# A planned instruction order in an SSM-convolution and gMLP kernel: four of six filler groups taken out, and a new order up to the first z tiles

## The chip, the core and the metric

The kernel runs on one core of one Trainium2 chip. The core has a matrix engine (TensorE, PE in the profile), a vector engine (VectorE, DVE), a scalar engine (ScalarE, ACT), a general engine (GpSimd, POOL) and SyncE (SP), which here only issues transfers. Each engine works through its own list of instructions in order; semaphores make one wait for another. Matmuls write to the accumulation memory (PSUM), and the other tiles lie in the on-chip memory (SBUF).

The metric is the device time of one execution, in microseconds. The kernel before takes 311.61 us, the median of three runs (311.52 to 312.55). A profiled execution of it took 311.07 us, and the span from its first to its last instruction is 309.2 us.

## What is computed

One block of a network, on 2048 tokens of width 640 in bf16. Cut to what matters:

```python
mod = (silu(c) @ w_mod).reshape(1, 6, 1, 640)      # sa, ca, ga, sb, cb, gb
h = layernorm(x) * (1 + ca) + sa
kv = shift_conv(k, shift_k) * v                    # 4 taps along the tokens
y = irfft(rfft(pad(kv)) * rfft(pad(ssm_k)))[:2048] + kv * ssm_D
x = x + ga * (h * y)
h = layernorm(x) * (1 + cb) + sb
z = gelu(h @ w_in)                                 # 2 x 864 columns
z1, z2 = z[..., :864], layernorm(z[..., 864:])
g = w_sp @ z2 + b_sp                               # over the 2048 tokens
x = x + gb * ((z1 * g) @ w_out)
```

## The kernel before

The first half (the modulation, the convolution and the first residual) is done in five blocks `u` of 128 columns. The Fourier transforms are matmuls with small tables that the kernel makes itself: M2 for the way forward and G2 for the way back. For each block there are:

- `taps` and `tv`: the four-tap convolution as matmuls with diagonal matrices (16 matmuls for 512 tokens), and DVE's product with v (line 560). K and V of the block are loaded into a `big` tile (`kv0` to `kv4`, two buffers).
- `s1` and `s1c`: the first stage of the transform, and its copies from PSUM. The tiles X1K are those of the filter, X1U those of kv.
- `fwd`: 8 forward stages each for the filter and for kv, of six matmuls. `khc` is ACT's copy of the filter's.
- `prod` (line 463): DVE's products of kv's and the filter's spectra. In half of the stages ("s" in MODE) two operations `csum` (line 477) add them up into W.
- `inv` and `zc`: the inverse stages, and their copies into Z.
- `zt`: a transposing DMA of Z into ZT, issued by SP. Block 4 is turned on PE instead (`zfl`, `zk`).
- `y` and `ym` (line 691), `yl` and `yml` (line 759) in block 4: the last stage, and its product with `gh`. `gh` is the first normalised x (`ln1`, `xn`), multiplied and added by `ghm` (line 674).
- `res` (line 711) adds `gh` to x, and `ln2` (line 717) takes the statistics of the second norm.

The second half works on four groups of 512 tokens. `ag2`, `rstd2`, `nmr2` and `zx` normalise, `hfl` and `hmod` turn and modulate the first group, `turn` and `hmod2` the other three, with a DMA. `zz` are the 64 z products of five matmuls, with `gelu` on ACT, and statistics and a norm of z2 (`stz`, `agz`, `zn`). Then `prodw` multiplies by w_sp, in Strassen's way with sums of halves (`ssum`, `tsum`). The first eighth of that stands in the ordered part; the other seven, with the output projection, follow in plain loops (from line 1160 on).

The ordered part is recorded first. Each step is handed to `op` (line 97), with what it reads and writes. It is one operation or a few, and may be allowed on several engines ("DG" is DVE or GpSimd). `Plan.run` (line 115) then goes through the text ORDER. There each word is an engine's letter (P, A, D, G for GpSimd, S for SP) and a step's number, so ORDER fixes both on which engine a step runs and the order of each engine's list. A step must not stand ahead of what it depends on. No time is in the text.

The modulation's weights `wm0` to `wm5` are loaded by SP into one buffer, one after another. The two halves of w_in (`ldwi`) take over `big` buffers.

The fillers are matmuls whose result is not used:

```python
        for i, k in enumerate(FILLS):
            def fill(e, i=i, k=k):
                p_ = new("fill%d" % i, "s1", [P, S1C, 2 * NJ * 4], F32)
                for j in range(k):
                    mm(p_[:, 0:2], ident[:], ident[:, None, :].to_broadcast([P, S1C, P]), j == 0, j == k - 1)
            op("P", "fill", fill, r=["ident"], w=["fill%d" % i], new=[("fill%d" % i, "s1")], n=k)
```

FILLS has the number of matmuls in each group, of 128 x 512. They are steps 1035 to 1040 before, the last recorded ahead of the final part, so that the steps behind them have numbers lower by four in the kernel after.

Of the kernel before, what the change touches and what calls it, by code (L numbers as in the profile page):

```python
# [30 lines left out]
PE_FLIPS = (4,)  # L31
TB = 4
NQ = DU // 4
FILLS = (4, 6, 2, 2, 4, 3, )
MODE = ('susussus', 'susussus', 'susussus', 'susussus', 'susussus')
SLOTS = dict(Tf=2, W=2, X=4, X1=4, KH=7, T=2, Z=3, ZT=1, wm=1, big=2, dg=2, st1=2, s1=1, sm=2, pu=2, pz=2)
PSUM_TAGS = ("s1", "sm", "pu", "pz")


ORDER = """  # L40
D0 D103 S91 G5 A4 P1035 D13 S2 G104 D105 D118 A1 P7 D119 A120 A10 D6 P8 A121 D106 S92 D14 A16 D107 S23 S25 A11 D94
A108 A109 D15 D17 D93 P1036 P148 A149 D112 D113 A114 G27 A115 D150 P151 G28 A152 P29 D18 D19 P31 P154 A153 A155 D30
D32 D124 G110 D125 A156 P157 A159 A158 D20 S24 P35 S26 D36 P33 D34 A127 A126 D130 G116 G117 G111 P160 A161 S526 G122
P139 D140 S95 D96 P166 A167 A131 P164 A21 D22 A165 G128 G129 P172 A173 G123 P168 A169 G42 P170 A171 D530 D531 S37 S38
P230 P174 A231 P142 P176 D532 P136 S527 A175 A178 A177 D143 G144 D137 P179 A180 P236 A237 S39 G41 S40 P182 G141 D181
A184 D183 P185 D187 A186 D533 P232 A233 P188 D189 P204 P1038 S52 P43 D205 G138 P198 D199 S529 G190 G191 P45 A534 A535
A536 P234 A235 P162 G55 D44 D46 P192 A193 P47 P49 D48 A163 P214 D132 D50 P206 A537 D215 P250 A251 G200 G201 G54 P202
S3 G81 P9 A12 P194 P145 A203 D545 D546 P224 G216 G217 P56 D195 D225 P1040 P1037 S51 P254 P220 A146 P60 A547 A255 D538
A207 P256 G147 A257 P208 P218 D221 G226 G227 S53 D57 A219 S568 P244 D209 G133 G134 A245 A548 P260 A261 D61 P58 D59
G539 D540 D556 D557 P238 P240 A239 P571 A572 S528 D541 D542 D543 S97 D98 G210 G211 P569 A570 P212 A213 P258 P62 P196  # L50
A259 P262 D263 S573 A241 P294 P222 D295 A197 P304 A544 D549 S65 D67 P228 D552 P248 A305 G68 A223 A249 D63 P576 P306
A307 P242 A243 G264 G265 P266 P252 A253 P574 D577 D553 D554 D555 P288 A229 A267 G550 D551 G560 G561 P310 G564 A311
P298 D575 D289 D299 D615 P296 P69 G290 S66 S64 P278 A558 D279 A562 G565 P308 P246 A297 P75 G291 G563 D70 P268 D269
S578 A309 A247 S99 D76 P328 G559 D654 A329 P318 A319 A566 P73 D74 S78 P272 D273 P330 A331 P324 G300 G301 G567 P579
D598 A325 P292 P332 A333 P326 S79 A327 P71 D712 D619 A293 D658 P316 S602 D652 D580 D620 D617 D100 D594 A317 D596 P334
A335 D80 G595 P282 D283 D274 G275 P270 A271 G597 G618 P280 A281 P312 A313 D599 D72 S77 P346 D347 P581 D582 P378 A379
G600 G601 P352 D353 P82 P302 A303 P380 A381 P314 A315 G284 D285 P336 D83 P84 P382 A383 P276 A277 P286 D85 D337 P322
P603 D338 D604 G710 A323 P384 A385 P320 A321 G339 S101 P368 A287 P605 G348 P340 P402 A403 G349 P372 D677 A341 P354
A355 D369 D606 P607 D373 G656 G657 D608 P390 G374 A391 P404 P362 P350 D375 A405 D363 P609 G616 P356 D357 D679 P406
A407 G659 G364 G365 D610 D611 P88 P388 A389 P408 A409 D102 A351 P342 D343 P370 S583 D371 A135 P400 A401 G621 P452 D680  # L60
P376 D89 A453 D622 P386 A387 P392 P86 D87 A377 G675 S623 A393 S90 P410 P456 P366 D411 A457 P398 G358 G359 A367 P624
D625 G612 A399 G412 P360 A361 P416 P454 A455 P420 D417 P626 D627 S759 G413 P414 A415 P394 A395 D421 P458 A459 P628
P344 A345 D629 P442 D443 P630 P476 A477 P430 D431 D432 G655 P418 A419 P396 A397 P482 P466 G613 A467 D631 A483 G422
G423 D642 D644 P446 D447 P424 P426 D427 G433 P434 A425 P478 P436 A479 G637 D641 G632 A435 D676 P444 A445 P460 P480
A481 P428 D437 D448 G449 A461 S660 D634 G653 P661 D662 D635 P474 D633 A429 P584 A475 P663 D664 P468 A585 P484 P450
A469 D485 P665 D666 G438 G439 A451 G673 G674 P440 P464 A441 A465 P500 D501 P667 G486 G487 P520 P488 A489 P504 P502
D521 P462 A463 G714 D505 D640 D668 S586 P587 P470 A471 A503 G522 G506 D507 G523 A588 P490 D491 S681 P510 D511 P508
P524 A509 P494 D495 P492 G711 G678 A525 G512 D513 P472 A493 P682 D683 A473 P516 D517 P514 A515 P684 D685 G496 G497
P498 A499 S760 P518 G669 D636 P686 G713 D638 D687 D639 A519 P722 D645 P688 D689 P718 P724 G670 P720 D719 P726 D721
G690 D691 D692 A723 A725 P728 P729 P727 D730 D731 S589 P592 D732 G695 D761 D733 D762 P1039 P738 D734 D735 P590 D694  # L70
D737 D775 A591 A593 G763 D764 D765 P752 D766 D736 D693 D774 P767 D769 D771 D770 P768 A773 D739 G776 D777 G779 P745
A772 P787 A778 P815 A788 D740 D741 D744 P781 D743 D699 D742 D697 A786 D840 A816 D698 D838 D696 D837 P821 P794 A795
D839 P780 G716 D717 D753 A822 G841 P819 D754 D842 G843 A844 G614 D671 P797 D845 P817 A798 D846 P790 G715 D782 A785
D784 D783 P808 A820 A818 A809 D746 D799 P804 A805 D747 D750 D643 D672 D700 A791 D703 D905 P827 P801 D702 D646 A802
A828 D704 D751 S847 G705 D706 D906 G647 D651 P829 D850 D749 D904 P825 A830 A848 D701 D748 A851 A826 G849 P823 A824
P811 A812 G852 S1042 D903 P881 G907 D908 D909 G910 D757 D813 D806 A882 P853 P856 A857 A854 P889 P883 A890 G912 S1048
D803 A884 P860 P891 A861 A892 P863 A864 P867 A868 D649 P870 D807 S1047 A871 D650 P885 D758 P877 A878 G911 S913 D755
D792 D1052 P895 A886 S1041 D708 D756 A918 A917 P874 A875 P893 P887 D971 A894 D709 D972 A896 D862 D648 D969 D1050 D707
D1053 D970 D789 D793 D865 G973 D974 A975 D976 G914 D915 D916 P933 P919 A934 D796 D800 P936 A888 A920 A937 G978 P943
A944 D1059 P940 P961 D810 D858 A941 P926 A927 A962 D855 D859 G977 S979 A981 P929 P951 D814 G831 D1057 D1058 G982 G984  # L80
D879 D832 D834 A930 A952 D1060 P955 A956 D869 A835 D872 S1045 D938 D935 D866 D939 P922 P949 A950 D980 D942 A923 G983
P1006 P985 A1007 D928 D876 D1049 D873 D921 D931 A986 S1043 P995 A996 D880 G897 P988 A989 D945 D946 D1054 D836 D833
D1065 D924 D898 D932 P1009 P992 D900 A993 D1008 D901 D925 G963 A1010 D987 D990 D1011 D1012 P999 A1000 D1001 D994 S1046
D964 P1002 A1003 D1004 D997 D998 P959 A899 A960 S1044 D991 P1027 D1061 A1028 P1015 A1016 D968 D1005 P947 G1029 A967
D966 A948 P957 A958 D902 P1017 D1066 D1030 D1034 P1023 A1033 A1018 A1024 D965 D1067 D1069 P953 A1031 D1032 D1068 P1073
A954 P1075 P1080 D1070 P1084 D1056 A1074 D1071 D1081 P1077 A1076 P1079 D1072 D1085 P1086 D1078 D1082 D1087 D1055 S1083
P1021 P1013 D1051 A1022 D1063 P1019 A1014 A1020 D1062 D1064 P1025 A1026 S1088
"""


# [39 lines left out]
def kernel(  # L130
# [79 lines left out]
    with ExitStack() as pctx:  # L210
# [748 lines left out]
        for g in range(NT // TB):  # L959
            z_group(g)  # L960
# [5 lines that stand above are left out]
# [258 lines left out]
```

## Time and profile before

| | |
|---|---|
| median of 3 runs | 311.61 us |
| profiled execution | 311.07 us |
| its span | 309.2 us |
| first filler matmul starts | 1.65 us |
| first z product starts | 134.01 us |
| the granted PE clock, mean | 0.999 |
| the w_in halves issued by SP | 94.5 and 117.9 us |

A share of busy time says how long an engine had an instruction running, and a matmul counts as running until its modelled end, which reaches into the next. Start-to-start distances in the timeline are nearer to what an instruction costs. In a line of groups, the first number behind the bar is the busy time and the second the mean duration of one, in ns; behind the second bar stands how long the engine was idle just before them.

### The profile page before, as it was taken

The numbers are of one execution on the slowest core, as the hardware profiler recorded it, in microseconds if no ns is written. First come the engines' busy times: TensorE is split into PE (matmuls) and PEld (weight loads), VectorE is DVE, ScalarE is ACT, GpSimd is POOL, SyncE is SP. The second block draws the span as 40 slices with busy tenths as digits, with TensorE's granted clock in tenths as the row PEclk, the third lists the DMA queues.
The fourth block names the chain that finished last, engine by engine and source line by source line (L and its number), as shares of the span: only waits on it lengthen the run. The fifth ranks groups of instructions, "written<-read, shape, count | busy, mean of one in ns | idle before, by whom it ended". The sixth has DMA issues, their size and how long they took to land.

```text
span 309.2 us, 6893 instructions
## 1 busy us (share of the span) xinstructions
PE 297.1 (96%) x2746; PEld 207.4 (67%) x2746; DVE 260.4 (84%) x531; ACT 156.5 (51%) x278; POOL 120.8 (39%) x152
## 2 busy tenths in 40 slices
PE   6888999999999999999999999999999999999996
PEld 1877888998989898765555555555565656555564
DVE  8999999999998999998799999967675858667473
ACT  4789899986899855466658767040101010010100
POOL 3537565958996698758526411000000000000000
PEclk9999999999999999999999999999999999999999
DMA  8889899998688869105875930093939395640714
GB/s 154 206 189 202 180 273 220 241 179 189 177 136 217 134 151 278 69 2 103 195 115 115 202 81 1 0 139 76 182 92 187 71 168 117 123 102 0 104 30 115
DMA packets 127091, 42.63 MB, mean 138 GB/s; under 512 B 116975, under 2 KB 127060, under 8 KB 127060
## 3 DMA queue, kind: packets, MB, share of 16 engines
q1 hardware_dynamic: 126906, 42.16, 66.3%
q8 instruction: 21, 0.34, 0.5%
q14 instruction: 10, 0.08, 0.1%
q10 hardware_dynamic: 154, 0.05, 0.1%
HBM read 16.11 MB, written 2.62 MB: 61 GB/s over the span
## 4 chain that ended last, share of the span: by engine, by line
PE 69%; DVE 23%; issue 3%; DMA 2%; POOL 2%; ACT 0%; DVEq 0%; POOLq 0%
PE ps L1026 23%; PE pu L244 13%; PE pz L244 11%; PE po L1150 10%; PE sm L244 5%; DVE Tf L463 4%; PE s L244 3%; DVE st L717 3%; PE pz L1026 2%; DMA wm<-in_w_mod_dram 2%; DVE gh L674 2%; PE pu L1026 1%; DVE T L463 1%; DVE xt L711 1%; DVE X L560 1%
## 5 line engine op out<-in xcount | busy, mean ns | idle before, releaser
L244 PEld LDWEIGHTS <-Z 128*128 128x128 bf16 x320 | 31.1, 98 | 27.3 <-DVE Z L910 0.5
L244 PE MATMUL pu<-X,M 128*128 128x128 bf16 (+1 forms) x480 | 46.5, 237 | 2.1 <-ACT KH L247 1.0
L244 PEld LDWEIGHTS <-M 128*128 128x128 bf16 x480 | 37.3, 98 | 6.1 <-issue 2.4
L1032 ACT COPY m<-ps 128x432 f32<-128x432 f32 x7 | 3.6, 518 | 72.7 <-PE ps L1026 72.7
L1026 PEld LDWEIGHTS <-S 128*128 128x128 bf16 x256 | 25.1, 98 | 21.7
L477 POOL TENSOR_TENSOR W<-Tf 128x256 bf16<-128x256 f32 x42 | 31.8, 772 | 13.4 <-DVE Tf L463 9.4
L247 ACT CAST X<-s 128x1024 bf16<-128x1024 f32 x32 | 32.5, 1017 | 6.9 <-PE s L244 6.8
L244 PE MATMUL pu<-big,Z 128*128 128x432 bf16 x160 | 33.3, 346 | 0.2
L1150 PE MATMUL po<-w_o,uT 128*128 128x320 bf16 (+2 forms) x231 | 32.7, 295 | 0.0
L244 PE MATMUL pz<-big,Z 128*128 128x432 bf16 x160 | 32.6, 346 | 0.0
L463 DVE TENSOR_TENSOR Tf<-pu,KH 128x1024 f32<-128x1024 f32 x25 | 30.1, 1213 | 0.6 <-PE pu L244 0.4
L1026 PEld LDWEIGHTS <-wT 128*128 128x128 bf16 x192 | 18.7, 98 | 15.2
L1150 PEld LDWEIGHTS <-uT 128*128 128x128 bf16 (+1 forms) x231 | 22.2, 98 | 9.7
L247 ACT CAST Z<-pz 128x512 bf16<-128x512 f32 x39 | 22.8, 593 | 7.1 <-PE pz L244 6.8
L244 PEld LDWEIGHTS <-G 128*128 128x128 bf16 x330 | 24.8, 98 | 2.1 <-issue 0.6
L247 ACT CAST KH<-pu 128x512 bf16<-128x512 f32 x40 | 23.4, 592 | 4.1 <-PE pu L244 4.1
L1026 PE MATMUL ps<-X,wT 128*128 128x432 bf16 x112 | 22.7, 346 | 0.0
L1026 PE MATMUL ps<-T,S 128*128 128x432 bf16 x112 | 22.7, 346 | 0.0
L244 PEld LDWEIGHTS <-X 128*128 128x128 bf16 x288 | 17.9, 97 | 5.5 <-DVE X L401 2.0
L1026 PE MATMUL ps<-X,S 128*128 128x432 bf16 x112 | 21.6, 346 | 0.0
L244 PE MATMUL sm<-dg,big 128*128 128x128 bf16 x320 | 20.7, 219 | 0.1
L463 DVE TENSOR_TENSOR T<-pu,KH 128x1024 bf16<-128x1024 f32 x15 | 18.2, 1213 | 1.6 <-PE pu L244 1.4
(187 smaller groups left out, 563.2 us busy)
## 6 DMA issues: line engine op xcount, KB each, us to landing
wm<-in_w_mod_dram SPq DMA_DIRECT2D x6, 800.0 KB, 5.4
xt<-in_A_q_dram SPq DMA_DIRECT2D x4, 640.0 KB, 6.0
out_dram<-ot SPq DMA_DIRECT2D x15, 160.0 KB, 2.1
big<-in_B_w_in_dram SPq DMA_DIRECT2D x2, 1080.0 KB, 7.1
X<-in_A_ssm_k_dram SPq DMA_DIRECT2D x4, 512.0 KB, 6.1
big<-in_A_v_dram SPq DMA_DIRECT2D x4, 512.0 KB, 6.3
w_o<-in_B_w_out_dram SPq DMA_DIRECT2D x6, 160.0 KB, 2.7
X<-in_A_ssm_k_dram SPq DMA_DIRECT2D x2, 256.0 KB, 3.4
```

What stands on the lines that cost most here:

```text
L244: nc.tensor.matmul(o, lhsT=w, rhs=x, start=start, stop=stop)
L247: (e.copy if e is nc.scalar else e.tensor_copy)(dst, src)
L463: e.tensor_tensor(T_[:], (tl[pu] if src is None else tl[src])[:, :, :, None, :].to_broadcast(shape), tl[KH][:, :, None, :, :].to_broadcast ...
L477: e.tensor_tensor(tl[W][:, :, o, :], T_[:, :, 0, o, :], T_[:, :, 1, 1 - o, :], op=ALU.add if o else ALU.subtract)
L560: e.tensor_tensor(tl[kv][:].rearrange("p c (n g) -> p n c g", g=8)[:, 4 * i:4 * i + 4], tl[ps][:].rearrange("p a (c g) -> p a c g", g=8), ...
L674: lambda e, vec=vec, o=o: e.tensor_tensor(gvu, gvu, vec[:, None, d0:d0 + du].to_broadcast([P, TB, du]), op=o),
L711: op("GD" if u < NU - 1 else "D", "res", lambda e: e.tensor_tensor(sl, sl, gl, op=ALU.add), r=[("gh", (u, g))], w=[("xt", (u, n)) for n in ...
L717: op("D", "ln2", lambda e, n=n: e.bn_stats(out=st2[:, n, (0, 0, 0, 1, 2)[u], :], in_=xt[:, n, us[0] * DU:(u + 1) * DU]), r=[("xt", (v, n)) ...
L1026: nc.tensor.matmul(ps[:, :FC], lhsT=lhs[:, s_, :], rhs=rhs(s_), start=(s_ == 0 and not more), stop=(s_ == HT - 1), skip_group_check=more)
L1032: nc.scalar.copy(part[p, m][:], part[p, BANK[m]][:, :FC])
L1150: nc.tensor.matmul(ps[:, :hi - lo], lhsT=uTs[t][:fsz[ft], ft, :], rhs=w_o[:fsz[ft], ft, lo:hi], start=(ft == 0), stop=(ft == NFT - 1))
```

## The change

It does two things. FILLS keeps the first two groups alone, so that 2, 2, 4 and 3 matmuls are gone. And ORDER is another one: most steps stand elsewhere, and some on another engine. Its first part, up to the first z tiles, was planned so that DVE's SBUF operations do not begin behind GpSimd's. The rest of the file is the same.

```diff
-FILLS = (4, 6, 2, 2, 4, 3, )
+FILLS = (4, 6)
 ...
-D0 D103 S91 G5 A4 P1035 D13 S2 G104 D105 D118 A1 P7 D119 A120 A10 D6 P8 A121 D106 S92 D14 A16 D107 S23 S25 A11 D94
-A108 A109 D15 D17 D93 P1036 P148 A149 D112 D113 A114 G27 A115 D150 P151 G28 A152 P29 D18 D19 P31 P154 A153 A155 D30
 ...
-D598 A325 P292 P332 A333 P326 S79 A327 P71 D712 D619 A293 D658 P316 S602 D652 D580 D620 D617 D100 D594 A317 D596 P334
 ...
-P498 A499 S760 P518 G669 D636 P686 G713 D638 D687 D639 A519 P722 D645 P688 D689 P718 P724 G670 P720 D719 P726 D721
-G690 D691 D692 A723 A725 P728 P729 P727 D730 D731 S589 P592 D732 G695 D761 D733 D762 P1039 P738 D734 D735 P590 D694
 ...
+A4 A1 D103 S91 S2 D0 S92 S23 G27 S25 G104 P1035 D105 D118 D119 A121 A120 P7 G5 D6 P8 A11 A10 D13 D14 A16 P1036 A28
+D106 D107 A108 D93 D15 D17 P148 A109 A150 A149 P151 D94 A152 A153 D112 D113 A115 A114 P29 P31 P157 D124 A158 D18 D125
 ...
+D580 D595 D597 A562 A563 S602 A333 P312 A313 P324 A131 D132 A325 P334 A335 P581 D100 P326 A327 G567 D621 D622 G284
+D285 P316 A317 D619 P276 A303 D598 D599 P378 A379 P352 P336 P270 D600 G601 G658 D353 S79 A277 D337 P380 A381 P346 D347
 ...
+A591 P592 S760 A593 P767 D769 D770 D771 D740 P768 A772 A773 P745 P797 D741 D743 D777 A778 D696 D699 D744 P794 A779
+P787 A795 A798 D697 D698 G717 D753 P781 A785 A786 D839 G671 P790 G614 D837 D742 D838 D840 P780 A791 D784 D782 D783
```

Steps named in what follows: S602 is the transposed load of ZT0, S79 the load of V for `kv4`, S78 that of its K, S99 a load of the filter's block 3; S760 loads the half of w_in for z1, S589 the last modulation weights; P787 and P797 are z products.

The steps that stand on another engine, in the whole order:

| step | before | after |
|---|---|---|
| `ghm` | 18 on DVE, 22 on GpSimd | 22, 18 |
| `xn` | 6 DVE, 7 GpSimd, 3 ACT | 0, 14, 2 |
| `zx` | 6 DVE, 7 GpSimd, 3 ACT | 6, 4, 6 |
| `zc` | 39 ACT, 1 DVE | 37, 3 |
| `zn` | 11 DVE, 5 ACT | 9, 7 |
| `ln1` | 9 DVE, 7 ACT | 8, 8 |
| `s1c` | 44 ACT, 4 DVE | 43, 5 |
| `gcopy` | 3 DVE, 1 ACT | 4, 0 |
| `diag` | 5 GpSimd | 3 GpSimd, 2 ACT |
| `mneg` | 4 GpSimd | 3 GpSimd, 1 ACT |
| `hmod2` | 4 DVE, 6 GpSimd, 5 ACT | 4, 5, 6 |

`csum` and `res` keep their numbers on each engine, but not the same steps.

## The prediction

> **What bounds the kernel now.** I read the page first, then busy time by stages, then the chain of waits around the seam between the stages, then single instructions.
>
> ```profile
> span 309.2 us, 6893 instructions
> PE 297.1 (96%) x2746; PEld 207.4 (67%) x2746; DVE 260.4 (84%) x531; ACT 156.5 (51%) x278; POOL 120.8 (39%) x152
> PEclk9999999999999999999999999999999999999999
> 0.00:134.00 134.00, 125.08 (x1737) 109.80 (x1738) 127.03 (x244) 104.20 (x183) 92.93 (x120) 1.00 0.85 184
> 134.00:204.00 70.00, 69.82 (x394) 37.31 (x391) 65.01 (x169) 43.77 (x82) 27.92 (x33) 1.00 0.52 95
> 204.00:309.20 105.20, 102.17 (x624) 60.32 (x621) 68.36 (x121) 8.50 (x15) 0.00 (x0) 1.00 0.54 107
> ```
>
> The last three lines are stages; their columns are busy PE, weight load, DVE, ACT, POOL, granted clock, DMA share, GB/s. I cut at 134.0 because the timeline has the first z product of the MLP (five matmuls, `zz`) start at 134.01. From there PE runs without a hole over 0.3 us to 203.9, where the ordered part ends, and the rest of the code is the same in both kernels. So **the change is worth what it does to the start of the first z product**, unless it opens holes after it.
>
> Before 134.0 PE and DVE both look full, which needs a second look.
>
> ```profile
> 130.82 0.29 DVE xt L711
> 131.92 0.71 DVE Z L860 x2
> 133.63 0.72 DVE Z L884 x2
> 142.25 1.12 POOL gh L674
> 147.91 1.45 DVE st L717 x5
> 150.15 1.64 PE pu L244 x8
> ```
>
> This chain of waits (start, length, what) says that what releases PE at the seam is DVE: normalising and modulating the first tokens, then the second group's. For PE I added what matmuls cost by their start-to-start steps: 80 forward stages of 0.44 (35.2), inverse stages 25 x 0.44 + 15 x 0.88 (24.2), 20 taps of 0.89 (17.8), 40 first stages of 0.436 (17.4), 8 modulation rows of 0.68 (5.4), the 21 fillers of 0.2135 (4.5), the rest 12.5: **117.0 us of PE work** before 134.0. It starts at 1.65 and loses 3.9 us before 10 us; 11.4 us more are lost later. DVE, likewise: 40 products of 1.13 (45.2), 20 taps x V of 0.60 (12.0), 16 y products of 0.59 (9.5), nine statistics of 0.99 (8.9), and so on: **117.9 us of DVE work**, from 1.3. DVE's other 14.8 us are two things: 8.6 us by which single operations are longer than the shortest of their kind, and 6.2 us of gaps and short delays.
>
> ```profile
> L674 DVE TENSOR_TENSOR gh<-gh,gca_bf 128x512 bf16<-128x512 bf16 x12 | 4.8, 436 | 0.0
> L674 DVE TENSOR_TENSOR gh<-gh,gsa_bf 128x512 bf16<-128x512 bf16 x5 | 4.0, 795 | 0.0
> 105.80 1.17 DVE L674 TENSOR_TENSOR gh<-gh,gsa_bf 128x512 bf16<-128x512 bf16 x1
> 105.54 1.15 POOL L674 TENSOR_TENSOR gh<-gh,gsa_bf 128x512 bf16<-128x512 bf16 x1
> ```
>
> The first two are groups (count, busy, mean ns): the same shape takes 436 or 795 ns. The last two show why: DVE's began at 105.80, 0.26 us after GpSimd's, and ended 0.28 us after it, in 1.17 us instead of 0.41. That is the loss the new order is about.
>
> **The change part by part.**
> *Fillers.* Eleven of 21 go: 2 at 25.7, 5 at 36.2, 4 at 129.2. By the step, 11 x 0.2135 = 2.35 us of PE work; PE's floor falls to 117.0 - 2.35 = 114.7. They also fill waits: after the five at 36.2 PE still waited 0.4 us, so a part turns into waiting. From nothing to 2.35; I take it together with the order below. The Trainium skill, "TensorE: Matmul & The Clock Gate" (Part 1: The HAM clock gate), speaks against taking them out: an idle window of about 3.4 us halves the clock. Row: the granted clock is 1.00 throughout, the filler's step is 427 ns at 5 us and 216 at 25.7, and the largest hole that the cut can leave is five fillers and their waits, 36.2 to 37.7, 1.5 us. By the row it costs 0; by the rule, if waits merge with it into a cold window, an estimated 1.7 us (3.4 us at half speed) each time. I take 0.
>
> *Operations that change engine before the first z product.* DVE takes 22 modulations of gh instead of 17 (+5 x 0.34 = 1.7), two more Z copies (+1.2), one G copy and one X copy (+1.15), two more residuals (+0.84), one yml (+0.6); it loses six normalisations to GpSimd (-6 x 0.35 = -2.1), one token tile's statistics (-1.0) and three tiny steps (-0.6), two zx (-0.7), two ln2 (-0.65). Sum +0.4: **118.3**. GpSimd's sum goes from 92.6 to 88.5, ACT's from 98.4 to 100.3 (two of its new operations are diagonals of four small copies, with no row on ACT: 0.8 to 2 us each by its steps of 0.21 for the small cosines and 0.48 for half-bank copies, I take 1; it stays 18 us below DVE). Neither sets the end.
>
> *Order.* For each DVE result that a PE stage needs I add DVE's work up to it and PE's work after it. Before, the tightest is the X1U0 copy ahead of the first forward stage of kv: 1.3 + 21.5 + 102.0 = 124.8. After it is 1.3 + 20.3 + 99.6 = 121.2, since the ln1 statistics stand behind the copies and fillers are gone. **Floor -3.6 us**. The actual start lies 9.2 above the floor now (134.0 - 124.8), of which much is the 8.6.
>
> *The stretched operations.* DVE operations with both inputs in SBUF (8 W sums, 17 gh modulations, 4 residuals, 6 additions of D) number 35 before the first z product, with 5.0 of the 8.6 us of stretch, 0.14 each. The new order has 42 of them. The Trainium skill, "SBUF — State Buffer" (Who interferes with whom), says that the pair of ports is an exclusive lock: whichever begins second blocks fully if GpSimd's operation reads SBUF. By that rule, with GpSimd busy 93 of 134 us and half of an operation of about 1.1 us left on average, unplanned would be 42 x 0.69 x 0.55 = 15.9 us (an estimate); by the row 42 x 0.14 = 5.9, and 9.5 with the rest. If the plan holds on the chip, near 0. The listed order doesn't show it: for 26 DVE operations (20 before) it has a GpSimd operation so shortly ahead that by the steps it would still run. Ends: 0 to 15.9; by the nearest row it would be 9.5, and I take half of the 8.6, 4.3, since a plan that separates them can be kept only as far as its starts don't drift.
>
> *SP's queue.* The transposed load of ZT0 moves ahead of the V load of kv4. That load is issued at 64.13 now, ZT0's at 64.75 and holds the queue 7.26 us.
>
> ```profile
> 64.13 0.57 SPq L522 DMA_DIRECT2D big<-in_A_v_dram  x1
> 64.75 7.26 SPq L698 DMA_TRANSPOSE ZT<-Z  x1
> 72.12 1.77 SPq L572 DMA_TRANSPOSE X<-X  x1
> ```
>
> SP now waits until 59.43 to issue X's load ahead of kv4's K; that load is put behind K, so SP can go on from wm0 at 56.7 with K (4.2) and X (0.4) to 61.3, and ZT0 holds it to 68.6, at the latest to 72.0. V lands 4.9 (median) later, 73.5 to 77. Its reader on DVE, at 74.55 now, would come at about 73. Cost 0 to 4 us; behind it on DVE stand all the products. I take 0.5. Of the others, the second w_in load goes behind wm5, needed five z products later (landing 7.1 us; issued about 118, cover 5 us): 0, at most 1. The wm chain (one buffer) is loaded as late as now or later, each about 1 us before its use: 0 to 1.
>
> *After the first z product.* PE has 69.9 us as now. DVE is busy 65 of 70 there, the second group was the late one at 150 (0.28 us). Its DVE work ahead is 131.0 against 130.7, PE's 129.8 against 132.2: it will wait by what DVE still loses, 0 to 2; I take it inside the sum.
>
> **Sum.** DVE: 1.3 + 118.3 + 4.3 + 6.2 = 130.1, against 134.0: -3.9; the V wait +0.5: -3.4, close to the floor's -3.6, got another way (PE's 114.7 and its start of 5.6 leave it 10 us for waits, 11.4 now). Against the profiled execution (311.07 us: span 309.2 and 1.9 around it) that is 307.7; the median of the runs is 0.5 above it, 311.6, so **308.2**.
>
> **Rivals.**
> 1. *The plan holds fully*: stretch 0, -4.3 more; PE's limit, 1.65 + 3.9 + 114.7 = 120.3, is not reached. -7.7: 303.9. For it: the 17 long operations are each over 100 ns, easily avoided. Against it: the list.
> 2. *Only fillers become waits*: stretched operations land elsewhere, DVE's 118.3 is no less than 117.9, so the seam stays at 134 +- 0.7: 311. For it: DVE's work is the same.
> 3. *Slower: the V load of kv4.* SP reaches ZT0 at 64.75 as now, V is issued at 72.0 and takes the 6.5 us of its slowest row: 78.5. DVE, 2 us earlier than now, stands at 72.5 and waits 6.0. Nothing covers it. With the other terms at the row (stretch 9.5, +0.9, and +0.4 of work; the fillers then only fill that wait): +7.3 less the 2 us it had gained and the 2 us of gaps of DVE that the wait swallows: +3.3, 315. It decides from a wait of about 3 us on. Against it: V's median is 4.9 and the new order frees SP earlier.
> That the order does not do what it says is 2 and 3.
>
> **How the numbers follow.** Forecast 0.42 (306 to 310), rival 1 0.18, rival 2 0.12, rival 3 0.28. What can be told from no change is 0.3%, 0.9 us. Faster: 0.42 + 0.18 + 0.01 of rival 2 = 0.61; same 0.09 of it; slower the rest of it and rival 3, 0.30. The range takes rival 1 and reaches to the lower half of rival 3: 302.8 to 314.2.
>
> **What would show it.** The start of the first z product: 130.6 (126.3 with rival 1, 134 with 2, 137 with 3). Of the mean of `gh<-gh,gsa_bf` on DVE: below 500 ns if planned. A DVE wait on the V load at 72 to 79: rival 3. A filler's or matmul's step of twice its length after 10 us: the clock. A hole of over 1 us in PE behind the first z product would make my stage cut wrong.

## The result, and the profile after

The kernel after takes **309.35 us**, the median of ten runs (307.41 to 310.79), where the kernel before took 311.69 in ten runs beside them (311.17 to 312.55). The ratio is 0.9922, with a 95% interval of 0.99 to 0.9944: faster, by about 0.8%. The profiled execution took 309.03 us. Its runs lie further apart than those of the kernel before, 3.4 us against 1.4.

The page of the kernel after (span; busy time; the clock by slices):

```profile
span 306.9 us, 6880 instructions
PE 294.1 (96%) x2735; PEld 206.3 (67%) x2735; DVE 255.9 (83%) x525; ACT 161.9 (53%) x292; POOL 115.3 (38%) x148
PEclk9999999999999999999999999999999999999999
```

PE's share is 96% as before, because the span shrank with the work. In this execution the clock stayed at 1.00. It did not in all of the ten: six have a mean granted clock of 0.999 or 1.000 (median 308.98 us), four have 0.994 (309.95). What lies behind that is told with the fillers below. Where the time went is seen from the stages, in the same columns as above (us from and to; length; busy PE, weight load, DVE, ACT, POOL; granted clock, DMA share, GB/s):

```profile
0.00:131.00 131.00, 121.74 (x1727) 108.52 (x1727) 122.07 (x239) 104.44 (x190) 90.13 (x119) 1.00 0.89 189
131.00:200.00 69.00, 68.12 (x382) 36.36 (x379) 63.53 (x163) 47.87 (x86) 25.15 (x29) 1.00 0.49 93
200.00:307.00 107.00, 104.20 (x635) 61.40 (x633) 70.34 (x125) 9.58 (x17) 0.00 (x0) 1.00 0.52 108
```

The first cut stands at 131.0 because the first z product now starts at 130.99 us, **3.0 us earlier** than at 134.01. DVE was busy 122.1 of the 131.0 us ahead of it, 5 us less than the 127.0 of before. In the second stage PE is busy 68.12 of 69.0 us, where it had been 69.82 of 70.0: holes have appeared there.

The groups that the prediction named, in the stage ahead of the first z product (count | busy us, mean ns of one | idle before):

```profile
L674 DVE TENSOR_TENSOR gh<-gh,gca_bf 128x512 bf16<-128x512 bf16 x12 | 4.8, 415 | 0.0
L674 DVE TENSOR_TENSOR gh<-gh,gsa_bf 128x512 bf16<-128x512 bf16 x10 | 4.4, 444 | 0.1
```

The second group had a mean of 795 ns and is at 444; there are ten of them now instead of five. The plan held on the chip: gate modulations hardly ever begin behind GpSimd's.

What came in its place on DVE is a wait for x (engine, line and tile waited for: us, times, longest), and SP's queue shows why:

```profile
DVE st L593 <- DMA xt<-in_A_q_dram: 1.7, 1, 1.7
```

```profile
23.80 6.96 SPq L525 DMA_TRANSPOSE big<-in_A_k_dram  x1
...
31.86 4.59 SPq L572 DMA_TRANSPOSE X<-X  x1
36.50 0.91 SPq L633 DMA_DIRECT2D wm<-in_w_mod_dram  x1
37.47 0.52 SPq L579 DMA_DIRECT2D xt<-in_A_q_dram  x1
```

Start and length of what SP issues: two transposing loads hold it for 7.0 and 4.6 us, then come the modulation's weights, and only at 37.47 the third quarter of x. That is 1 us earlier than before (38.42), but DVE reached the statistics that read it earlier still. Before, DVE had no wait here.

And ACT's timeline at the seam shows two causes of the holes:

```profile
132.97 1.73 ACT L856 ACTIVATE Z<-xt,nmr,rstd 128x640 bf16<-128x640 bf16 x2 [1.54 <-DVE nmr L846]
134.72 1.28 ACT L933 ACT_TABLE_LOAD   x1
136.02 0.53 ACT L933 ACTIVATE X<-pu 128x432 bf16<-128x432 f32 x1
```

The table for the GELU is loaded at 134.72, between the first z product and the first `gelu`. In the kernel before a step of its own (135, `gelut`) loaded it at 88.03 us, where ACT had time, by a GELU of one column:

```profile
88.03 1.28 ACT L805 ACT_TABLE_LOAD   x1
```

The new order has A135 among the z products, behind the first 18 `gelu` steps, so that the first of these has to load the table itself.

The other cause is the line at 132.97. By the steps of the timeline PE has three holes there, of 0.91, 0.27 and 0.35 us. The first waits for the normalised second pair of token tiles, the other two for the first `gelu` steps (PE's waits, 131 to 140 us):

```profile
PE sm L871 <- ACT Z L856: 0.6, 1, 0.6
PE pu L244 <- ACT X L933: 0.2, 1, 0.2
```

Before, ACT and GpSimd normalised that pair side by side, and it was done 2.1 us behind the start of the first z product. Now ACT does both tiles, one after the other, and it is done 3.7 us behind it.

### The profile page after: what moved, and what is told of

Its sections match the earlier page's. It is cut to its first block, busy times and chain, and to the rows that moved or that the text cites. A ratio compares the mean times of both kernels' runs of the same rounds, so it can differ in the third digit from the quotient of the medians.

```text
span 306.9 us, 6880 instructions
## 1 busy us (share of the span) xinstructions
PE 294.1 (96%) x2735; PEld 206.3 (67%) x2735; DVE 255.9 (83%) x525; ACT 161.9 (53%) x292; POOL 115.3 (38%) x148
## 4 chain that ended last, share of the span: by engine, by line
PE 74%; DVE 14%; DMA 6%; ACT 3%; issue 1%; POOL 1%; DVEq 0%; SPq 0%; POOLq 0%
PE ps L1026 23%; PE pu L244 15%; PE pz L244 14%; PE po L1150 10%; PE sm L244 5%; PE s L244 3%; DVE Tf L463 3%; DMA ZT<-Z 3%; DMA X<-X 2%; PE pz L1026 2%; PE pu L1026 1%; DVE st L717 1%; POOL W L477 1%; DVE st L593 1%; DVE X L560 1%
## 5 line engine op out<-in xcount | busy, mean ns | idle before, releaser
L244 PE MATMUL pu<-X,M 128*128 128x128 bf16 (+1 forms) x480 | 44.9, 237 | 1.4 <-DVE X L247 0.3
L244 PEld LDWEIGHTS <-M 128*128 128x128 bf16 x480 | 36.6, 98 | 5.2 <-issue 1.9
L244 PE MATMUL pu<-big,Z 128*128 128x432 bf16 x160 | 32.6, 346 | 0.3 <-ACT X L933 0.2
L247 ACT CAST Z<-pz 128x512 bf16<-128x512 f32 x37 | 21.9, 596 | 3.3 <-PE pz L244 2.9
L244 PEld LDWEIGHTS <-big 128*128 128x128 bf16 x320 | 18.8, 98 | 0.7 <-issue 0.6
```

The lines of the kernel that those rows point to most:

```text
L244: nc.tensor.matmul(o, lhsT=w, rhs=x, start=start, stop=stop)
L247: (e.copy if e is nc.scalar else e.tensor_copy)(dst, src)
```

## The experiments

**How they are compared.** Two numbers of each profile stand beside the time: the start of the first z product, and the *stretch* of DVE ahead of it, the sum of what its operations took beyond the shortest of their kind (over 0.12 us each; a kind is a line with its tiles and shapes). In this table and in the text that shortest one is taken over all kernels of the table, and so the kernel before has 10.1 us of it. The prediction's 8.6, and the 9.7 of the kernel before without fillers in an expectation, were taken over fewer kernels. The column before the last is the rest of the span behind the first z product; the last one has the number of runs with a mean granted clock of 0.995 or less.

| kernel | median us (runs), ratio to before, 95% | span | first z | stretch | from first z to the end | clock 0.995 or less |
|---|---|---|---|---|---|---|
| before | 311.69 (10) | 309.2 | 134.01 | 10.1 | 175.2 | 0 of 61 |
| after | 309.35 (10), 0.9922, 0.9900 to 0.9944 | 306.9 | 130.99 | 4.5 | 175.9 | 4 of 10 |
| before, no filler groups (e1) | 311.77 (12), 1.0008, 0.9998 to 1.0017 | 310.5 | 135.11 | 11.2 | 175.4 | 4 of 12 |
| after, with filler groups (e2) | 310.01 (6), 0.9950, 0.9933 to 0.9967 | 308.5 | 132.57 | 4.5 | 175.9 | 0 of 6 |
| after, table early (e3) | 308.88 (6), 0.9916, 0.9898 to 0.9933 | 305.7 | 130.16 | 4.6 | 175.6 | 1 of 6 |
| before, three moved (e4) | 310.40 (5), 0.9967, 0.9954 to 0.9980 | 308.8 | 133.42 | 9.5 | 175.4 | 0 of 5 |
| after, table and loads early (e6) | 310.01 (12), 0.9953, 0.9929 to 0.9976 | 309.0 | 133.90 | 4.6 | 175.1 | 8 of 12 |
| after, once more (e7) | 309.09 (6), 0.9927, 0.9908 to 0.9946 | 306.7 | 130.73 | 4.3 | 175.9 | 0 of 6 |
| after, table early, once more (e8) | 308.81 (5), 0.9915, 0.9901 to 0.9929 | 307.2 | 131.82 | 4.1 | 175.4 | 1 of 5 |
| table early, a sum moved (e9) | 309.09 (5), 0.9921, 0.9908 to 0.9935 | 306.9 | 131.54 | 3.7 | 175.4 | 1 of 5 |
| after, three put behind (e10) | 309.77 (12), 0.9937, 0.9914 to 0.9959 | 307.6 | 131.63 | 5.2 | 175.9 | 5 of 12 |
| before's order, after's engines (e11) | 327.95 (6), 1.0532, 1.0506 to 1.0557 | 324.7 | 149.54 | 13.3 | 175.1 | 6 of 6 |
| after's order, before's engines (e12) | 330.05 (5), 1.0608, 1.0584 to 1.0631 | 328.2 | 152.22 | 14.5 | 176.0 | 5 of 5 |

e1 to e4 ran on one chip with the same runs of the kernel before (median 311.58), likewise e7 to e10 (311.47), and e11 and e12 (311.18); e6 ran beside 17 others (311.58). The 61 of the first row are these runs of the kernel before, together.

### The two halves of the change, each alone

e1 takes the four filler groups out of the kernel before and leaves its order. e2 puts them back into the kernel after.

```diff
-FILLS = (4, 6, 2, 2, 4, 3, )
+FILLS = (4, 6)
 ...
-P1037 P1038 P1039 P1040
```

(The words stand at four places of ORDER; e2 is the reverse, and each group stands ahead of or behind the same step as before.)

> The order of before, with the four filler groups taken out and nothing moved. Theory (order): the gain comes from fewer stretched DVE operations, and fillers only stand in time in which PE would wait for DVE anyway, so 311.7 us within 0.6, the first z product at 133.5 to 134.2. Rival (fillers): their 11 x 0.2135 us are work on the path, and the kernel gains 1.5 to 2.4 us, 309.3 to 310.2, which would be all of the change's gain; the first z product then at 131.7 to 132.5.

> The changed kernel with the four filler groups put back, next to the same neighbours where these still follow each other (2 matmuls at about 24 us, 5 ahead of the first stage of block 1's kv, 4 ahead of the second group's last stage at about 125 us). Theory (order): no more than 0.7 us slower than the changed kernel, 309.3 to 310.0. Rival (fillers): 1.5 to 2.4 us slower, 310.9 to 311.7, as slow as before.

**The fillers alone are worth nothing in the median**: 311.77 against 311.58 us, ratio 1.0008. PE lost 18.8 us in waits ahead of the first z product instead of 15.4: more than the 2.35 us of matmuls came back as waits. DVE had nothing less to do, and lost 1.1 us more by stretches, since everything that shifted a little met GpSimd elsewhere. Two of DVE's modulations, which had taken 0.41 and 0.55 us before, in the timeline of this kernel (start, length):

```profile
57.66 0.94 DVE L674 TENSOR_TENSOR gh<-gh,gca_bf 128x512 bf16<-128x512 bf16 x1
...
62.37 1.04 DVE L674 TENSOR_TENSOR gh<-gh,gca_bf 128x512 bf16<-128x512 bf16 x1
```

The first z product came 1.1 us later, as much as the stretch had grown. In the new order the fillers do cost something: with them the first z product is 1.6 us later and the median 310.01 against 309.09 to 309.35 (the second pair in other batches, with intervals that overlap). So **the order carries the gain**, and the cut is worth at most some 0.9 us on top of it.

The fillers did one thing that the medians hide: **they kept the clock up**. In all 72 runs with the six groups (the kernel before, e2 and e4) the mean granted clock is 0.998 or more. Of the 68 runs of after, e1, e3 and e6 to e10, which lack four groups, 24 have 0.989 to 0.995. e1 differs from the kernel before in the fillers alone, and has four of 12 against none of 61. What such a number is, the trace of e6 shows, whose profiled run has 0.989 (stages, the same columns):

```profile
36.61:40.02 3.41, 1.08 (x18) 0.94 (x16) 1.24 (x2) 1.32 (x4) 1.40 (x3) 1.00 1.22 133
40.02:43.43 3.41, 3.41 (x27) 2.92 (x25) 3.31 (x10) 1.50 (x2) 2.10 (x3) 0.50 0.97 294
128.77:132.18 3.41, 2.36 (x62) 1.82 (x59) 3.24 (x13) 1.14 (x3) 1.91 (x4) 1.00 0.00 0
132.18:135.59 3.41, 3.41 (x47) 2.43 (x47) 3.34 (x11) 1.61 (x5) 3.24 (x5) 0.50 0.00 0
```

For two stretches of 3.41 us the granted clock is 0.50, behind stretches in which PE was busy for only 1.08 and 2.36 us. One stretch at half the clock in a span of 307 us makes the mean 0.994 (1 - 0.5 x 3.41 / 307), two make it 0.989. The second lies at the seam, where the four fillers at 129.2 used to stand. The kernel before and the kernel after at that time:

```profile
128.76:132.18 3.42, 3.42 (x72) 2.62 (x70) 3.21 (x14) 0.45 (x2) 1.40 (x3) 1.00 0.02 5
128.76:132.18 3.42, 2.63 (x48) 2.01 (x49) 3.32 (x12) 2.40 (x5) 3.25 (x5) 1.00 0.00 0
```

Laid anywhere at the seam, 3.41 us hold at least 3.12 us of busy PE in the kernel before, 2.57 in e1 and 2.36 in the kernel after. Where the clock fell in the four runs of the kernel after is still not shown, as the trace that was kept is of a run at 0.999, and what exactly the clock goes by is open. By the medians a run with such a stretch is 1.0 us longer in the kernel after (309.95 against 308.98) and 0.5 us in e1 (311.91 against 311.38).

### The table load

e3, and e8 beside a second batch of the kernel after (e7), have one word moved:

```diff
-P400 A401 D677
+P400 A135 A401 D677
 ...
-P883 A884 A135 S1043
+P883 A884 S1043
```

> The changed kernel with one ACT step moved: the one that brings in the Gelu table stands where it stood before (about 88 us, between copies) and not behind the first two gelus. Theory (table): the 1.28 us load at 134.7 us is what holes PE between 134 and 138.8 us (1.5 us lost there against 0.5 before); gone, the kernel gains 0.7 to 1.3 us, 308.0 to 308.7, and the load on ACT at about 86 us is covered. Rival (first tokens late): PE waits there for the normalised second pair of token tiles, which DVE hands to ACT at 132.97, and the load only lies in that wait: no change within 0.3, or ACT, which is busier at 86 us, passes the delay on.

> The changed kernel once more, so that the next three can be compared with it on the same chip. Theory and rival alike expect 309.0 to 310.0 us, a ratio to the kernel before of 0.992 to 0.995.

> The changed kernel with the exact-GELU table loaded early (step 135 back ahead of step 401), beside the changed kernel itself. Theory (the 1.28 us table load behind the first z product lies on the chain): 0.5 to 1.0 us less than the changed kernel in the same runs. Rival (TensorE finds other work meanwhile or loses the time later): within 0.3 us of it.

ACT's timeline of e8 at the same place:

```profile
133.79 1.73 ACT L856 ACTIVATE Z<-xt,nmr,rstd 128x640 bf16<-128x640 bf16 x2 [1.53 <-DVE nmr L846]
135.43 0.51 ACT L933 ACTIVATE X<-pu 128x432 bf16<-128x432 f32 x1
```

The first `gelu` follows the normalisation at once. The medians moved by 0.5 us (e3, another batch) and 0.3 us (e8), less than expected, and the intervals overlap. Here the time from the first z product to the end is the better measure, as it leaves out what happens ahead of it. In the five kernels with the late table (after, e2, e7, e10, e12) it is 175.9 to 176.0 us; in the eight with the early one 175.1 to 175.6. Not one crosses over. Four of the eight have the order of before behind the seam too, and e6 has its low clock there, so the fair ones are e3, e8 and e9, with 175.4 to 175.6. **The misplaced load costs about 0.5 us**, the difference of the means (175.94 against 175.46). PE's steps say the same: in e8 the holes of 0.27 and 0.35 us are gone, and that of 0.91 us is still there. The rest of the 1.28 us is hidden. That e8's whole time fell by less has a cause ahead of the first z product, which was 1.1 us later than in e7. There the two have the same order until ACT's table load at 83.6 us, and yet the load of block 2's K held SP's queue for different times, in e7

```profile
23.84 5.43 SPq L525 DMA_TRANSPOSE big<-in_A_k_dram  x1
```

and in e8

```profile
23.88 6.56 SPq L525 DMA_TRANSPOSE big<-in_A_k_dram  x1
```

so that x's third quarter came later and DVE waited 3.1 us for it instead of 1.9. This spread comes with the loads and not from the edit.

### The loads between 22 and 44 us

e6 is e3 with two loads moved up: the third quarter of x (step 528) ahead of block 2's load of V (step 53), and the small load of c (step 3) ahead of its load of K (step 52).

```diff
-S52 D54
+S3 S52 D54
 ...
-P194 S3 D46
+P194 D46
 ...
-P214 S53 D195
+P214 S528 S53 D195
 ...
-G553 S528 D541
+G553 D541
```

> The changed kernel with three steps moved: the Gelu table as in the run before, the load of the third quarter of x ahead of the V load of block 2 (31.4 instead of 37.5 us on SP's queue), and the small load of c ahead of the transposing load of block 2's K (about 23.8 instead of 30.9). Theory (the saved stretch is spent in waits on loads): DVE's wait of 1.7 to 1.9 us at 42 us and PE's of 0.7 at 33 go, and 1 to 2 us come off the run with the Gelu table alone: 306.9 to 307.9. Rival (PE is the bound there, or the loads moved ahead delay block 2's): 308.9 within 0.4, or slower.

The wait for x is gone, and another stands there. Waits of DVE and of PE in e6:

```profile
DVE X L560 <- DMA big<-in_A_v_dram: 3.3, 1, 3.3
```

```profile
PE sm L244 <- DVE X L560: 2.5, 2, 2.3
```

Block 2's V, 0.5 MB, now lands behind x's 0.64 MB. DVE's product with it waits 3.3 us, PE waits 2.5 us for that product, and the first z product is at 133.90. So in these two orders of the loads **whichever load goes last is the one waited for**, once DVE is quicker. Only this one other order was tried; whether another is better is open.

The wait costs more than itself. The hole that it leaves in PE (37.19 to 39.52) is the one behind which the clock fell above, and so 133.90 holds both. Eight of e6's 12 runs have a clock of 0.994 or less, with a median of 311.05 us; the other four have 308.99, near e3's 308.88.

### Which operations stand behind each other

e5 computes nothing of the kernel and writes zeros. It runs eight kinds of DVE operation, each behind nothing, behind a GpSimd addition of two SBUF tiles, behind a GpSimd operation on one tile (`tensor_scalar`), and behind a GpSimd `memset`, GpSimd's beginning 0.09 to 0.16, 0.14 and about 1.06 us ahead.

```diff
+    tests = (
+        lambda: v.tensor_tensor(y[:, 0:512], x1[:, 0:512], x2[:, 0:512], op=ALU.mult),
 ...
+    loads = (
+        lambda: None,
+        lambda: g.tensor_tensor(gb[:, 0:512], g1[:, 0:512], g2[:, 0:512], op=ALU.add),
+        lambda: g.tensor_scalar(gb[:], g1[:], sc[:, 0:1], sc[:, 1:2], op0=ALU.mult, op1=ALU.add),
+        lambda: g.memset(go[:], 0.0),
+    )
```

> Leaves out the whole computation and writes zeros. Eight forms of DVE operation (two SBUF inputs in bf16 of 512 and in f32 of 256; one SBUF and one PSUM input; a tensor_scalar with two scalar columns in bf16 of 640; the statistics of 256; two tiny f32 steps of 8; a cast from PSUM), each begun about 0.2 to 0.3 us behind a GpSimd operation: none, one with two SBUF inputs, one with one SBUF input, one that only writes. Theory (lock by the form): the two-input forms and the tiny f32 ones take 0.5 to 1.0 us longer behind a reading GpSimd operation and nothing longer behind one that only writes; the forms with one SBUF input from PSUM and the statistics take the same in all four. Rival (any SBUF operation waits behind any GpSimd operation): all forms with an SBUF operand, the statistics too, are longer behind all three. Open: the tensor_scalar in bf16, which the trace of before shows once at 840 ns and otherwise at 434 to 446.

| DVE operation, ns | alone | GpSimd, two tiles | GpSimd, one tile | memset |
|---|---|---|---|---|
| tensor_tensor, SBUF and SBUF, bf16 512 | 415 | 1339 | 415 | 414 |
| tensor_tensor, SBUF and SBUF, f32 256 | 415 | 1339 | 415 | 413 |
| tensor_tensor, PSUM and SBUF | 680 | 680 | 680 | 680 |
| tensor_scalar, bf16 640 | 436 | 1240 | 2665 | (429) |
| statistics | 417 | 416 | 419 | 416 |
| tensor_scalar, f32 of 8 | 161 | 1084 | 164 | 771 |
| scalar_tensor_tensor, f32 of 8 | 156 | 1079 | 156 | 154 |
| copy from PSUM | 680 | 680 | 680 | 680 |

(Medians of three. The operation in brackets began when the memset was over.) Three pairs of the timeline show it directly:

```profile
8.04 1.15 POOL L55 TENSOR_TENSOR gb<-g,g 128x512 bf16<-128x512 bf16 x1 [7.60 <-ACT g L63]
8.20 1.27 DVE L43 TENSOR_TENSOR y<-x,x 128x512 bf16<-128x512 bf16 x1
...
10.05 1.14 POOL L56 TENSOR_SCALAR gb<-g,sc 128x640 bf16<-128x640 bf16 x1 [0.86 <-ACT go L62]
10.19 0.41 DVE L43 TENSOR_TENSOR y<-x,x 128x512 bf16<-128x512 bf16 x1
...
30.75 0.88 POOL L56 TENSOR_SCALAR gb<-g,sc 128x640 bf16<-128x640 bf16 x1 [0.86 <-ACT go L62]
30.89 2.67 DVE L46 TENSOR_SCALAR y<-x,sc 128x640 bf16<-128x640 bf16 x1
31.57 1.80 POOL L57 MEMSET go<- 128x2048 f32 x1
```

In the first pair DVE ends 0.28 us after GpSimd. In the second, GpSimd's normalisation form (one tile and two scalars) does not hold up this DVE operation at all. In the third, DVE's wide tensor_scalar waits through GpSimd's and through the next one as well: between two GpSimd operations that follow each other at once it isn't let in.

The kernels agree for the wide sums, modulations and residuals. In the 13 profiles of the table, 62 of DVE's began at least 0.06 us behind a GpSimd sum, modulation or residual that had over 0.3 us to go. **All 62 were stretched**, by 0.4 to 1.0 us on average, depending on the pair. Behind any other GpSimd operation 24 began, and none was stretched. But two tiles are not the whole rule: of these 24 only two are behind a normalisation, and 21 are behind the last step of `rstd` (line 190), which reads two tiles as well, of two to eight columns.

Nor do GpSimd's operations on one tile leave all of DVE's alone. In all nine profiles of the new order a table step of DVE with two tiles is stretched behind GpSimd's `gneg` (line 376, which changes the sign of a table), from 0.41 to 1.16 us. In eight of the nine a small two-tile step of the statistics is stretched behind a normalisation (line 621), from 0.16 to 0.58 us. The timeline of the kernel after:

```profile
16.55 1.05 POOL L376 TENSOR_SCALAR G<-G 128x1024 bf16<-128x1024 bf16 x1 [1.66 <-DVE G L247]
16.70 1.16 DVE L301 TENSOR_TENSOR F1bdU<-f1cU,gmaskU 128x256 bf16<-128x256 f32 x1
...
52.07 0.87 POOL L621 TENSOR_SCALAR gh<-xt,rstd,nmr 128x640 bf16<-128x640 bf16 x1
52.37 0.58 DVE L605 TENSOR_TENSOR mv<-mv,sums 128x4 f32<-128x4 f32 x1
```

What sets these apart from e5's second pair was not tested; e5 has about one distance between the two starts for each pair. So the six normalisations that moved to GpSimd held up none of DVE's sums and modulations in the new order, but a step of its statistics, by 0.4 us. GpSimd has 65 sums, modulations and residuals ahead of the first z product instead of 70.

### Is the stretch the currency?

Three small doses. e4 moves three stretched operations of the kernel before to places where GpSimd is free. e9 moves one stretched sum of the kernel after (step 448, 1.37 us at 103.39). e10 moves three modulations back behind GpSimd's.

The three moves of e4, the one of e9 (beside the early table) and the three of e10:

```diff
-D617 D100 D594
+D617 D100 D599 D594
-D375 A405 D363
+D375 A405 D102 D363
-A479 G637 D641
+A479 G637 D676 D641
```

```diff
-P480 D448 P428
+P480 P428
-G612 D638 P434
+G612 D638 D448 P434
```

```diff
-G658 D353 S79
+G658 D353 D599 S79
-P410 D411 S623
+P410 D411 D656 S623
-A451 D664 D485
+A451 D664 D714 D485
```

> The order of before, with three DVE steps moved to where GpSimd has nothing running by the trace: the gh modulation of 69.6 us ahead of the one at 66.96, the one of 105.80 ahead of the statistics at 105.47, the addition of D of 87.6 ahead of the product of 83.2. Nothing else is changed; their stretch is 1.01 + 0.76 + 0.99 = 2.8 us on DVE. Theory (lock on the path): the three take 0.41, 0.41 and 0.2 us, and the first z product comes 1 to 2.8 us earlier, 309.0 to 310.7 in all. Rival (DVE is not what counts there): they are shorter and the time stays 311.7 within 0.5.

> The same, and one column sum of VectorE (step 448, 1.37 us where it lies behind GpSimd's residual at 103 us, 0.4 us by itself) moved behind step 638, where no GpSimd operation with two SBUF inputs runs. Theory (what a stretched operation loses ahead of the first z product comes back one for one): stretch 3.5 us instead of 4.5, and 0.5 to 0.9 us less than the run with the early table alone. Rival (another operation is caught instead, as when three were moved in the kernel before): stretch 4 us or more, within 0.3 us of that run.

> The changed kernel with three of VectorE's gate modulations put back to where a GpSimd operation with two SBUF inputs begins just ahead of them (steps 599, 656 and 714). Theory (the order frees VectorE from GpSimd, and that is the gain): stretch 6.5 to 7.5 us instead of 4.5, first z product 2 to 3 us later, 310.9 to 312.4 us, 1.5 to 3 us more than the changed kernel. Rival (the gain is from elsewhere in the order, or others come free): within 0.3 us of the changed kernel.

None of the doses came out at the size that was meant. In e4 the two modulations were freed (0.41 and 0.42 us), the addition of D only in part (0.76 us instead of 1.17), and others were caught, so that the stretch fell by only 0.6 us. The timeline of e4:

```profile
84.45 1.16 POOL L674 TENSOR_TENSOR gh<-gh,gsa_bf 128x512 bf16<-128x512 bf16 x1
85.60 0.97 DVE L674 TENSOR_TENSOR gh<-gh,gca_bf 128x512 bf16<-128x512 bf16 x1
87.11 2.45 POOL L674 TENSOR_TENSOR gh<-gh,gca_bf 128x512 bf16<-128x512 bf16 x2
87.20 1.35 DVE L711 TENSOR_TENSOR xt<-xt,gh 128x512 bf16<-128x512 bf16 x1
```

In e10 the starts drifted too, and the stretch grew by 0.8 us over e7, not by 2 to 3. One of the three turned the tables:

```profile
107.76 0.42 DVE L674 TENSOR_TENSOR gh<-gh,gca_bf 128x512 bf16<-128x512 bf16 x1
107.79 1.40 POOL L674 TENSOR_TENSOR gh<-gh,gca_bf 128x512 bf16<-128x512 bf16 x1
```

DVE came 0.03 us first, and it was GpSimd that took 1.40 us instead of 1.15. GpSimd can be the one that waits.

What did come out agrees in size. Stretch and first z product moved by +1.1 and +1.1 us (e1 against before), -0.6 and -0.6 (e4 against before), -0.3 and -0.3 (e9 against e8), +0.8 and +0.9 (e10 against e7; 0.6 of that 0.9 may be a longer wait for x, 2.5 us against 1.9). The times do not follow as closely. Only e4 is clear, at 0.9967 (0.9954 to 0.9980), which is 1.2 us for a dose of 0.6; e1's median grew by 0.2 us for 1.1; e9 and e10 lie within the intervals of the kernels they are compared with. So a small dose of stretch seems to be worth itself up to the first z product. That rests on single profiles, and the times do not show it.

### Who does it, and when

The order changes both the engine of a step and its place. e11 is e1 with the 42 steps that change between DVE and GpSimd on the engines of the kernel after; e12 is the kernel after with these on the engines of before.

```diff
-D617 D552 G595
+G617 G552 D595
 ...
```

(Three of the 42 words as e11 has them; e12 is the reverse, in the other order.)

> The kernel before without its four filler groups, in its own order, but every VectorE or GpSimd operation ahead of the first z product on the engine that the changed kernel gives it (six normalizations, a residual, padding and half of the gate modulations change sides). It tells the two halves of the new order apart: which engine does an operation, and when. Theory A (the shares do it: fewer GpSimd operations with two SBUF inputs, so fewer stretches): stretch 7 us or less against 9.7, first z product at 133 or before, ratio to the kernel before 0.997 or less. Theory B (the times do it: an operation starts ahead of GpSimd's, not behind it): stretch 8.5 us or more, first z product at 134.5 or later, ratio 0.999 or more.

> The other corner: the changed kernel in its new order, with the same operations back on the engine that the kernel before gave them. Theory A (the shares do it): stretch 7 us or more against 4.5, first z product 133 or later, ratio to the kernel before 0.997 or more. Theory B (the times do it): stretch 5.5 us or less, first z product at 132 or before, ratio 0.995 or less. If both halves are needed, both runs lie near the kernel before.

e11 lies on the side of theory B and e12 on that of theory A: neither the engines nor the places alone keep the gain. But that both would lie near the kernel before is wrong by far: they are **5.3% and 6.1% slower**. The two halves are no separate gains to be added. The modulations of e11 (up to its first z product), which are spread over the engines as in the kernel after:

```profile
L674 DVE TENSOR_TENSOR gh<-gh,gca_bf 128x512 bf16<-128x512 bf16 x11 | 6.8, 640 | 0.0
L674 DVE TENSOR_TENSOR gh<-gh,gsa_bf 128x512 bf16<-128x512 bf16 x10 | 5.8, 600 | 0.0
```

640 and 600 ns against 415 and 444 with the same shares: what keeps them apart is the place. But the stretch of these two, 2 and 10 us more than in e1 and in after, is the smaller part of a first z product that comes 14 and 21 us later. The rest is waiting, as an operation on another engine comes due at another moment, and the clock: e11's trace has two stretches of 3.41 us at 0.50, e12's has four. At half speed each is at most 1.7 us of PE work. How the rest divides was not worked out. In e12 (stages; the same columns), around a hole:

```profile
60.00:71.90 11.90, 11.71 (x147) 10.58 (x145) 8.73 (x13) 11.50 (x19) 9.79 (x12) 1.00 1.04 197
71.90:77.50 5.60, 0.60 (x8) 0.39 (x6) 5.57 (x8) 1.50 (x2) 2.91 (x3) 0.98 0.90 252
77.50:81.00 3.50, 3.50 (x31) 3.22 (x31) 3.43 (x5) 0.02 (x1) 0.33 (x1) 0.55 0.00 0
```

DVE is busy 5.57 of 5.60 us and PE waits 5.0 us for its product. In the 3.5 us behind the hole, PE's granted clock is 0.55.

## Why the prediction was right, and where its sizes were off

The direction was right, and so was the mechanism: the fall of the time is that of the first z product's start, less a loss behind it. The forecast was -3.4 us, the medians say -2.3. By the steps:

- **The fillers, "from nothing to 2.35", taken with the order.** Right to have no term of their own: alone they brought 0 (e1). For the clock the prediction took 0, and that is a term that it mis-sized. It held in the profiled execution; in four of the ten runs a stretch of 3.41 us at half the clock shows in the mean, and these were 1.0 us longer, where the estimate by the rule was 1.7 each time. The prediction asked for waits that merge to 3.4 us, and looked at the place at 36.2. In e6 the clock fell with PE busy for 1.08 and 2.36 us of the 3.41 ahead, and the four fillers at 129.2 stood at the seam, where PE is now least busy.
- **DVE's work +0.4.** Measured +0.3, by the sum of DVE's durations less stretch.
- **The stretch: "I take half of the 8.6", so -4.3.** Measured -5.5, on the wider base. The term was too small, and only some 3.0 us of it are where the prediction looked: its sums, modulations, residuals and additions of D fell from 5.0 to 2.0 us, nearly all of that in the modulations and the additions. Another 2.4 us are in DVE's table steps ahead of 20 us, which fell from 3.7 to 1.3. The estimate by the rule, 15.9, took all of GpSimd's busy time as dangerous. By e5 and the pairs of the traces a part of its operations is not, the normalisations for wide sums and modulations among them. Rival 1 (stretch 0, 303.9 us) fell: 4.5 us are left, of which 1.0 is the sum at 103 us (1.37 us long) and 0.6 the residual at 96.
- **The "6.2 us of gaps and short delays", carried over unchanged.** This is the first term that was mis-sized: DVE's waiting grew by 2.2 us. 1.7 of that is the wait for x's third quarter, which the profile of before could not show as a wait, as DVE came too late to wait. The prediction asked what a faster DVE would meet next at one place, kv4's V, and not at this one.
- **V of kv4, 0.5.** Measured 0. The time at which SP would issue it was worked out as 68.6, and it was issued at 68.63; DVE had no wait for it. Rival 3 fell with that.
- **The first z product at 130.6.** 130.99: +0.3 - 5.5 + 2.2 = -3.0. That the time came so near is luck: two errors, of 1.2 and 2.2 us, and V's 0.5 almost cancelled here. That the floor had given -3.6 as well was not tested by any run.
- **"After the first z product", 0 to 2 inside the sum.** This is the second one: 0.7 us outside the sum (175.2 to 175.9). It wasn't DVE, as the step had it, but ACT. About 0.5 of it is the table load. The step counted what changes engine and what moves on SP, and it did not go through ACT's list, on which a 1.28 us load had moved from where it was hidden to where a z product waits for its `gelu`. The other 0.2 us is not traced to one cause; the hole of 0.91 us, behind two normalisations that now stand on ACT one after the other, is a part of what PE loses there. PE's z products take 70.0 us from the first to the last start, and 69.0 before. No single hole was over 1 us; the three sum to 1.5.

With -3.0 and +0.7 the span falls by 2.3 us, as measured (309.2 to 306.9).

Rival 2, with fillers that become waits and stretches that land elsewhere, is not what the change did. It is a fair description of e1.

## What to carry to other kernels

When one engine's delays are taken out, go through every transfer and table load that it used to reach late: a load that shows no wait may have been only just in time, and a small step that moves on an engine off the path counts as well. A planned order is one piece: moving an operation to another engine at the same place in the order, or to another place on the same engine, shifts everything behind it, and here half of the plan was worth minus 5%. To keep VectorE free of GpSimd, look at the forms: wide operations on two SBUF tiles on both sides are to be kept apart, while VectorE's statistics and PSUM reads can lie beside GpSimd's operations. For GpSimd's one-tile operations look at the durations of the pair at hand: some were harmless here and some were not. And when fillers are taken out, read the granted clock of every run, not only that of the profiled one.

## What the runs showed of the hardware, unexpectedly

- In e5 a two-tile DVE operation waits behind a two-tile GpSimd operation (415 to 1339 ns) and not behind a one-tile one (415). In the kernels one waits behind a one-tile `gneg` as well (0.41 to 1.16 us), and none behind the small two-tile step of `rstd`. A wide one-tile tensor_scalar of DVE waits behind both forms in e5, and, between GpSimd operations in close order, through two of them (2665 ns for 436).
- A tiny tensor_scalar (f32 of 8) waited even behind a memset (771 ns for 161), where scalar_tensor_tensor of that size did not (154).
- TensorE's granted clock fell to 0.50 for 3.41 us at a time: twice in the trace of e6, twice in e11's, four times in e12's. In e11 four of the five PE stages behind a hole of 3.4 us took 0.85 us from start to start instead of 0.44, 1.65 us lost. The Trainium skill, "TensorE: Matmul & The Clock Gate" (Part 1: The HAM clock gate), has half the clock after an idle window of about 3.4 us, and the prediction's estimate from it was 1.7 us. The half and the length agree. The condition does not: of the eight times PE was idle for all of the 3.41 us ahead in one (e12), and busy for 0.43 to 2.36 us of them in the seven others.
- One and the same transposing load held SP's queue for 5.43, 6.56 and 6.96 us in three runs of the same order up to there.
